# Two lanes of a matmul filler that share a PSUM bank in turn, with a new planned order

## The chip, the cores and the metric

One core of a Trainium2 chip. The metric is the device time of one execution in microseconds (us), as a median over runs. Engines are named as the profile names them: PE (TensorE matmul), PEld (TensorE weight load), DVE (VectorE), ACT (ScalarE), POOL (GpSimd), SP (SyncE, which here issues every transfer).

## The reference

An attention layer and a gated layer run on the same x (2048 rows of 512) and are mixed row by row:

```python
q = (x @ wq), 32 heads of 16;  k = x @ wk;  v = x @ wv      # one k and v for all heads
a = softmax(q k^T / 4) v @ wo
b = (sigmoid(x @ w_gate) * (x @ w_up)) @ w_down             # F = 1792
g = sigmoid((x * gate_w).sum(-1))
out = g * a + (1 - g) * b
```

All is float32. To keep that precision with fast matmuls the kernel splits numbers into a high and a low float32r part and adds three products (high x high, high x low, low x high).

## The kernel before, in words

Rows of x come in 4 blocks (b) of 512. Attention is done in 32 units (u): a block and 4 heads. A unit has 64 matmuls for the row maxima of the scores (kind m, `maximum`, line 1092, reduced by DVE in line 1094), 64 for the scores themselves (kind s, `scores`, line 1101; ACT's exp in line 1103 makes a tile p), and 16 value steps V (`pv`, line 977): four f32 matmuls of 32 columns each, one from each of four p tiles. The maxima of a unit are turned by one small TensorE step T (`max_turn`, line 963) and sent by SyncE into the rows 62, 63, 126 and 127 of the queries (`send_max`, line 970), so that the scores come out with their maximum taken off. `load_q` (line 951) loads a unit's queries in six transfers.

m and s use only 64 rows of the array, so TensorE is split into two **lanes**, rows 0 to 63 and 64 to 127, which run two matmuls at once. Each step of that kind is a *pair slot*. The rest of the work fills the free lanes (kind f, `fill`, line 1071): the gated layer's gate (g) and up (u) products, its down product (d), and the attention's output product (a, at the end e). Each such job is one output tile, or two, in PSUM; there are 8 banks, held by whatever works in them.

Before the change each lane works in a bank of its own:

- For g and u a job is 256 columns of F; lane h makes columns h. It needs all 512 rows of the product's inner dimension and has only 64 partitions, so it also needs the other half of x's rows on its own partitions. `turn_x` (lines 775 to 781) sends x's halves across into tiles xs, by two transfers for each two chunks.
- For d and a a job is one tile of 128 rows of the output. Each lane adds up its half of the inner dimension, so one tile ends in two banks. `part_of` (line 1040) takes them out: the first copy goes to the tile ba by ACT ("first"), later ones go to ACT and then a POOL add (`add_part`, "apart", lines 1052 and 1055), or to a DVE sum onto ba ("sum", line 1034).

After a unit's value steps, `finish` (line 984) copies the bank to ou or, when the run of V steps was cut short, to a partial sum that POOL adds (`add_sums`, line 991). Then SyncE handles the softmax's denominators: `store` (lines 999 and 1002) writes the row of sums to memory and moves the four heads' 16 rows into vd, `sums` (line 1006) reads the sums back, DVE inverts them, `send_inverse` (line 1014) and `spread` (line 1019) send the inverses over 64 rows, POOL multiplies.

**What sets the order.** A string, `ORDER`, is played through a planner (`State`, lines 101 to 640) that keeps a clock and each engine's load, and writes the list of operations in which all engines then stand. A hexadecimal digit is a pair slot (a lane does nothing, m, s or f), V and T are as above, G is a step of the first projections (128 rows), a dot is a short pause. TensorE changes its form between pair slots and the steps V, T and G; the planner books that with `IN` and `OUT`. SP's transfers stand where the planner thinks that their data is there. All engines work through their lists in order, and only semaphores hold them up.

Of the kernel before, what the change touches and what calls it, by code (L numbers as in the profile page):

```python
# [30 lines left out]
RAW, WB, DB, PB, HB, BA_BUFS = 2, 2, 4, 21, 6, 4  # L31
# [19 lines left out]
IN, OUT, VALUES, TURN = 52, 94, 371, 60  # L51
# [9 lines left out]
LATER = (("load_x", 2), 8000), (("load_x", 3), 8100), (("turn_x", 0, 0), 12200), (("turn_x", 0, 1), 12300)  # L61
FEED_AT = 13700
# [11 lines left out]
class Job:  # L74

    def __init__(self, kind, b, i, n, items=()):
        self.kind, self.b, self.i, self.n = kind, b, i, n

        self.items = items

        self.group = (kind, b, i // NT if kind == "d" else 0 if kind == "a" else i)
        self.key = (kind, b, i)

# [5 lines left out]
def block_jobs(b):  # L89
    out = []  # L90

    def ds(gi):
        f0, f1 = FG[gi]
        items = [("d", b, f) for f in range(f0, f1)]
        if gi == len(FG) - 1 and b + 1 < NB:
            items[1:1] = [("x", b + 1, i) for i in range(KC // 2)]
        return [Job("d", b, gi * NT + t, 6 * (f1 - f0), items if t == 0 else ()) for t in range(NT)]

    for gi, (f0, f1) in enumerate(FG):
        for f in range(f0, f1):  # L100
            out.append(Job("g", b, f, 24, [("g", b, f)]))
            if f == f0 and 0 < gi < len(FG) - 1:
                if gi == 1 and b:

                    out += [Job("a", b - 1, t, 3 * KC, [("a", b - 1, i) for i in range(KC // 2)] if t == 0 else ())
                            for t in range(NT)]
                out += ds(gi - 1)
            out.append(Job("u", b, f, 24, [("u", b, f)]))
# [3 lines left out]
class State:  # L112

    def __init__(self):
# [11 lines left out]
        self.job, self.at, self.bank = [0, 0], [None, None], [None, None]  # L126
# [9 lines left out]
        self.parts, self.out = {}, {}  # L136
        self.x_done = [0] * NB
        self.x_ready, self.x_loaded = [NEVER] * NB, [BEGIN[0], X1_THERE, NEVER, NEVER]
# [19 lines left out]
    def send(self, n, kb):  # L158

        self.on("sp", self.now, n * ISSUE)  # L160
        self.on("dma", self.sp, kb * TEN_KB // 10)
# [40 lines left out]
    def run(self, t):  # L202
# [28 lines left out]
        elif what == "x":  # L231
            self.after(at, "turn_x", *args)
# [12 lines left out]
    def divided(self, u, at):  # L245
# [3 lines left out]
        if u == NU - 2:  # L249
            self.jobs += [Job("e", b, t, 3, [("e", b, 0)] if t == 0 else ()) for t in range(NT)]  # L250
        elif u == NU - 3:
            new = [Job("a", b, t, 3 * (KC - 1)) for t in range(NT)]
# [21 lines left out]
    def event(self, what, args):  # L274
# [7 lines left out]
        elif what == "turn_x":  # L282
            b = args[0]
            self.x_done[b] += 1
            at = self.send(2, 1024)
            if self.x_done[b] == KC // 2:
                self.x_ready[b] = at
        elif what == "send_max":
            self.max_ready[args[0]] = self.send(4, 16)
        elif what == "store":  # L290
            at = self.sums_free[args[0] % OU] = self.send(5, 136) + SAFE
            self.after(at, "sums", *args)
        elif what == "sums":
            self.after(self.send(1, 8) + 2 * SAFE, "invert", *args)
# [4 lines left out]
        elif what == "spread":  # L299
            u = args[0]  # L300
            at = self.send(1, 128)
# [59 lines left out]
    def begins(self, h):  # L361
# [7 lines left out]
        if j.kind == "d" and (j.b, j.i % NT) not in self.parts and min(self.tile_free) > self.now:  # L369
            return False  # L370
        return self.has(j, 0)

    def has(self, j, at):
# [3 lines left out]
        if j.kind == "d":  # L377
            f = FG[j.i // NT][0] + at // 6
# [3 lines left out]
    def can_f(self, h):  # L382
        if self.at[h] is None:
            return self.begins(h)
        return self.has(self.jobs[self.job[h]], self.at[h])

    def issue_f(self, h):
        if self.at[h] is None:
            self.bank[h], self.at[h] = self.take(), 0
        j = self.jobs[self.job[h]]  # L390
        self.acts.append(("f", h, j, self.at[h], self.bank[h]))
        self.at[h] += 1
        self.issued[h] += 1

    def settle(self):
        for h in range(2):
            while self.at[h] is not None and self.at[h] == self.jobs[self.job[h]].n:
                j = self.jobs[self.job[h]]
                second = self.halves.get(j.key, 0)
                self.halves[j.key] = second + 1  # L400
                at, i = self.now + LATE, self.bank[h]
                if j.kind == "g":
                    self.acts.append(("gate", h, j, i))
                    at = self.on("act", at, COPY)
                    tail = TAIL_A + FREE_A
                elif j.kind == "u":
                    slot, free = self.take_h()
                    self.acts.append(("gated", h, j, i))
                    at = self.on("dve", max(at, free), GATED)
                    tail = TAIL + FREE  # L410
# [789 lines left out]
```

## Time and profile before

| what | value |
|---|---|
| median of 3 timed runs | 1601.36 us (1601.09 to 1601.44) |
| the profiled execution, in all | 1598.83 us |
| its span, first to last instruction | 1597.1 us |
| TensorE clock granted | 1.000 |
| PE, busy | 1587.9 us (99%) |
| DVE, busy | 1392.0 us (87%) |
| ACT, busy | 1258.4 us (79%) |
| POOL, busy | 848.0 us (53%) |
| moved by DMA | 102.31 MB |

A PE row's duration includes the time in which a matmul shares the array with the next one; start times, not durations, tell what a step costs. SP is a queue only: its rows are transfers being issued and semaphores being waited for. L numbers are lines of the kernel.

### The profile page before, as it was taken

The page shows a single profiled execution, that of the slowest core. Times are in us where ns is not written, and L with a number is a line of the kernel's source. Part 1 is how long each engine was busy: PE and PEld are TensorE (multiplying, and loading weights), DVE is VectorE, ACT ScalarE, POOL GpSimd, SP SyncE. Part 2 cuts the span into 40 slices and gives each one's busy share as a digit, 9 for nine tenths or more (in the row PEclk, how much of TensorE's full clock was granted, in tenths as well). Part 3 has the DMA queues.
Part 4 walks back from the last instruction along what each step waited for, and adds up shares of the span by engine and source line. Part 5 has one row for each costly group of instructions (what it writes and reads, how often), then busy time and mean ns, then how long its engine had stood idle before and what let it go on. Part 6 is the DMA issues. An engine that isn't in the chain of part 4 may idle for free.

```text
span 1597.1 us, 33902 instructions
## 1 busy us (share of the span) xinstructions
PE 1587.9 (99%) x12918; PEld 998.6 (63%) x12918; DVE 1392.0 (87%) x2372; ACT 1258.4 (79%) x2474; POOL 848.0 (53%) x708
## 2 busy tenths in 40 slices
PE   9999999999999999999999999999999999999998
PEld 7776665665656566566666566666656665656654
DVE  7999998998988989988998898889989998988832
ACT  4268778888878878879878877878987887878896
POOL 4254364558363664375745446454936366536463
PEclk9999999999999999999999999999999999999999
DMA  7621121115111212013411121111502021201111
GB/s 239 216 80 42 42 57 36 45 59 137 29 68 32 75 56 60 18 39 83 111 37 58 39 75 54 55 38 59 137 28 68 32 75 46 71 16 42 34 36 44
DMA packets 54678, 102.31 MB, mean 64 GB/s; under 512 B 18232, under 2 KB 19768, under 8 KB 53492
## 3 DMA queue, kind: packets, MB, share of 16 engines
q1 hardware_dynamic: 54516, 100.16, 21.0%
q8 instruction: 101, 1.65, 0.4%
q14 instruction: 61, 0.50, 0.1%
HBM read 74.05 MB, written 13.09 MB: 55 GB/s over the span
## 4 chain that ended last, share of the span: by engine, by line
PE 98%; ACT 0%; DVE 0%; DMA 0%; POOL 0%; issue 0%; DVEq 0%
PE bank L1071 31%; PE bank L977 29%; PE bank L1092 18%; PE bank L1101 16%; PE bank L838 4%; ACT p L1103 0%; PE bank L963 0%; PE bank L908 0%; DVE ba L1148 0%; DVE ba L1034 0%; DMA wkv_raw<-wkv 0%; POOL wkv_s L732 0%; DVE wkv_stack L869 0%; PE bank L1144 0%; DVEq L1196 0%
## 5 line engine op out<-in xcount | busy, mean ns | idle before, releaser
L1094 DVE TENSOR_REDUCE mx<-bank 128x1 f32<-128x512 f32 x2048 | 1257.4, 681 | 133.8 <-PE bank L1092 80.5
L1103 ACT ACTIVATE p<-bank 128x512 f32<-128x512 f32 x2048 | 1050.1, 652 | 2.6 <-PE bank L1101 0.4
L1101 PE MATMUL bank<-qs,ks 64*128 64x512 f32 x2048 | 698.0, 400 | 0.0
L1092 PE MATMUL bank<-ks,qs 62*128 62x512 f32 x2048 | 686.6, 406 | 0.0
L977 PE MATMUL bank<-p,v_aug 128*32 128x512 f32 x4096 | 491.3, 598 | 0.7 <-ACT p L1103 0.7
L1092 PEld LDWEIGHTS bank<-ks,qs 62*128 62x128 f32 x2048 | 338.4, 184 | 151.3 <-issue 51.1
L1101 PEld LDWEIGHTS bank<-qs,ks 64*128 64x128 f32 x2048 | 345.7, 185 | 105.5 <-ACT p L1103 29.9
L991 POOL TENSOR_TENSOR ou<-ou,ou 128x512 f32<-128x512 f32 x201 | 259.0, 1289 | 204.9 <-ACT ou L984 199.2
L984 ACT COPY ou<-bank 128x512 f32<-128x512 f32 x232 | 140.9, 608 | 266.6 <-PE bank L977 122.2
L1071 PE MATMUL bank<-wd,hl 64*128 64x512 f32 x1344 | 273.5, 393 | 0.0
L977 PEld LDWEIGHTS bank<-p,v_aug 128*32 128x32 f32 x4096 | 107.7, 109 | 232.2 <-issue 188.1
L1071 PEld LDWEIGHTS bank<-wd,hl 64*128 64x128 f32 x1344 | 195.0, 185 | 20.4 <-ACT p L1103 1.7
L1071 PE MATMUL bank<-xs,wg 64*128 64x512 f32 x672 | 203.2, 393 | 0.0
L1071 PE MATMUL bank<-xs,wu 64*128 64x512 f32 x672 | 199.7, 393 | 0.0
L1071 PE MATMUL bank<-x,wu 64*128 64x512 f32 x672 | 194.5, 391 | 0.0
L1071 PE MATMUL bank<-x,wg 64*128 64x512 f32 x672 | 190.4, 391 | 0.0
L1071 PEld LDWEIGHTS bank<-xs,wg 64*128 64x128 f32 x672 | 119.7, 185 | 8.1
L1071 PEld LDWEIGHTS bank<-xs,wu 64*128 64x128 f32 x672 | 118.6, 185 | 7.3
L1071 PEld LDWEIGHTS bank<-x,wu 64*128 64x128 f32 x672 | 115.5, 185 | 10.7 <-issue 1.7
L1071 PEld LDWEIGHTS bank<-x,wg 64*128 64x128 f32 x672 | 113.3, 185 | 9.4 <-POOL wu L814 0.8
L1055 POOL TENSOR_TENSOR ba<-ba,pa_d 128x512 f32<-128x512 f32 x48 | 61.8, 1288 | 95.9 <-DVE ba L1034 62.6
L813 POOL CAST wu<-ru 128x1024 fp32r<-128x1024 f32 x27 | 28.1, 1039 | 117.6 <-PE bank L1071 94.3
(83 smaller groups left out, 1064.1 us busy)
## 6 DMA issues: line engine op xcount, KB each, us to landing
rg<-wg SPq DMA_DIRECT2D x28, 512.0 KB
ru<-wu SPq DMA_DIRECT2D x28, 512.0 KB
rd<-wd SPq DMA_DIRECT2D x28, 512.0 KB
qs<-qd SPq DMA_DIRECT2D x192, 64.0 KB
qd<-q SPq DMA_DIRECT2D x32, 256.0 KB
xs<-x SPq DMA_DIRECT2D x16, 512.0 KB
xf<-x_in SPq DMA_DIRECT2D x16, 256.0 KB
ra<-wo SPq DMA_DIRECT2D x8, 512.0 KB
```

Of the source, the lines that this page charges most:

```text
L813: nc.gpsimd.tensor_copy(WS[item][:, 0, :], raw)
L838: nc.tensor.matmul(ps, w[:, p, part(kc)], X[b, kc][:, q, :], start=i == 0, stop=i == 3 * KC - 1)
L977: nc.tensor.matmul(ps[32 * j:32 * j + 32, :], v_aug[:, c, :], PT.pop((u, c, j)), start=start, stop=stop)
L984: nc.scalar.copy(to, ps)
L991: nc.gpsimd.tensor_tensor(SUMS[u], SUMS[u], PARTS_OF[u].pop(0), op=ALU.add)
L1055: nc.gpsimd.tensor_tensor(BA[b, t], BA[b, t], PA.pop((b, t)), op=ALU.add)
L1071: nc.tensor.matmul(banks[i], l, r, start=at == 0, stop=at == j.n - 1)
L1092: nc.tensor.matmul(banks[i], qs_t[u % 3][r, pr, part(qt)], ks[r, kb * 512:(kb + 1) * 512], start=True, stop=True)
L1094: nc.vector.tensor_reduce(MX[u][:, pr, h, qt, kb:kb + 1], banks[i], axis=AX.X, op=ALU.max)
L1101: nc.tensor.matmul(banks[i], ks[r, part(c)], qs_t[u % 3][r, pr, :], start=True, stop=True)
L1103: nc.scalar.activation(p, banks[i], AF.Exp, scale=0.25)
```

## The change

Lanes now share banks. A job has two output tiles and two banks. Each lane first adds its 64 rows of the inner dimension into its own tile's bank, then *crosses over* and adds its half into the other's, without clearing it. So a lane needs only its own half of x, `turn_x` goes (and the host's layout of w_gate and w_up with it), and a tile of d or a ends in one bank.

A lane may not add into a bank while the other still does. The last matmul of a lane's first half and the first matmul after the crossing are tied by an empty SyncE instruction: it waits for the one, and the other waits for it. The planner books it (`TURN_OVER` on SP, `SEEN_OVER` behind that) and lets no lane cross before. `store` and `sums` use one transfer out to memory and one back for the four heads' rows, in place of four. The T step is a plain matmul with the identity, of 32 columns. There are 29 p tiles where there were 21, since the tiles xs are gone. The planner has new costs for the transfers, and the order string is a new one.

```diff
-RAW, WB, DB, PB, HB, BA_BUFS = 2, 2, 4, 21, 6, 4
+RAW, WB, DB, PB, HB, BA_BUFS = 2, 2, 4, 29, 6, 4
...
-IN, OUT, VALUES, TURN = 52, 94, 371, 60
+IN, OUT, VALUES, TURN = 52, 94, 371, 92
...
-FEED_AT = 13700
+FEED_AT = 12200
+TURN_OVER, SEEN_OVER = 40, 100
...
-        return [Job("d", b, gi * NT + t, 6 * (f1 - f0), items if t == 0 else ()) for t in range(NT)]
+        return [Job("d", b, gi * 2 + t, 6 * (f1 - f0), items if t == 0 else ()) for t in range(2)]
...
     def can_f(self, h):
-        if self.at[h] is None:
+        at, n = self.at[h], self.job[h]
+        if at is None:
             return self.begins(h)
-        return self.has(self.jobs[self.job[h]], self.at[h])
+        j = self.jobs[n]
+        if at == j.n and j.kind != "e" and self.now < self.half_end.get((n, 1 - h), NEVER):
+            return False
+        return self.has(j, at % j.n)
...
+        if at + 1 == j.n and not alone:
+            self.half_end[n, h] = self.on("sp", self.now + LATE, TURN_OVER) + SEEN_OVER
...
-    "GGGGGGG555G55G555.G551G554.G..G55G555G55GG555G55G5ff7ffddff7f5ffffff7fdff7ffdff5G55GTG555G577Gbfed9fedbf6fb7edeb"
+    "GGGGGGG555G55G555.G55........5G55GG555GGG555G55G555GG55G557G777fddfffdffdfd7GT7dffff7ffd75Gdefffdfe7edef6f6f9fbf"
...
-    def turn_x(b, i):
-
-        two = XR.pop((b, i))
-        xs = fp.tile([P, 2, 2, TB], F32R, tag="xs", name=f"xs{b}_{i}", bufs=KC // 2)
-        XS[b, 2 * i], XS[b, 2 * i + 1] = xs[:, 0], xs[:, 1]
-        nc.sync.dma_start(f32(xs[TOP]), f32(two[BOT]))
-        nc.sync.dma_start(f32(xs[BOT]), f32(two[TOP]))
...
-        nc.tensor.transpose(ps[:16, :P], mm, ident)
+        nc.tensor.matmul(ps[:32, :P], mm, ident, start=True, stop=True)
...
-        for j in range(4):
-            r = 64 * (u % 2) + DH * j
-            nc.sync.dma_start(VD[u // 2][0][r:r + DH, :], ou[32 * j:32 * j + DH, :])
+        SUMS[u] = dp.tile([4, TB], F32, name=f"sd{u}"), dp.tile([P, TB], F32, name=f"od{u}")
+        nc.sync.dma_start(SUMS[u][0], ou.rearrange("(j r) t -> j r t", j=4)[:, DH, :])
+        nc.sync.dma_start(SUMS[u][1], ou)
...
+        nc.sync.dma_start(rc, sd.rearrange("j (p c) -> (j p) c", c=DH))
+        r = 64 * (u % 2)
+        nc.sync.dma_start(VD[u // 2][0][r:r + 64, :], od.rearrange("(j r) t -> j r t", j=4)[:, :DH, :])
...
+    def after(one, other):
+
+        tc.add_manual_dep(one.ins, other.ins.name, mybir.DependencyInfo(
+            mybir.DependencyClass.Sync, mybir.DependencyReason.DATA), reason="a bank's other rows")
+
+    def fill(h, j, x, at, start, stop, i):
         c, (p, q) = at // 3, THREE[at % 3]
         half = HALF[h]
         if j.kind in "gu":
-            l, r = WS[j.key][half, p, part(c)], (X if c % 2 == h else XS)[j.b, c // 2][half, q, :]
+            l, r = WS[j.key][half, p, part(2 * c + x)], X[j.b, c][half, q, :]
...
-        nc.tensor.matmul(banks[i], l, r, start=at == 0, stop=at == j.n - 1)
+        ins = nc.tensor.matmul(banks[i], l, r, start=start, stop=stop)
+        if at == 0 and not start:
+            after(ins, CROSS.pop((j.key, x)))
+        elif at == j.n - 1 and not stop:
+            CROSS[j.key, x] = nc.sync.nop()
+            after(CROSS[j.key, x], ins)
```

First place: TensorE in block 1, at the end of the first down product's first half (wd is its weights, hl its input; L1139 and L1148 are m and s of the changed kernel, L1113 the filler). Before, both lanes end the same tile's two banks, 72 and 75, and wait for no one:

```order
L1071 MATMUL bank_72<-wd_1_1_6644,hl_3_5969 128x512
L1071 MATMUL bank_75<-wd_1_1_6644,hl_3_5969 128x512
L1071 MATMUL bank_72<-wd_1_1_6644,hl_3_5969 128x512
L1071 MATMUL bank_75<-wd_1_1_6644,hl_3_5969 128x512
L1092 MATMUL bank_76<-ks,qs_109 128x512 [waits DVE_49]
L1092 MATMUL bank_74<-ks,qs_109 128x512 [waits Activation_49]
L1101 MATMUL bank_77<-qs_107,ks 128x512 [waits Activation_49]
L1071 MATMUL bank_75<-wd_1_1_6644,hl_3_5969 128x512
```

After, bank 76 gets the last matmul of its first half in the first row here, and the other lane's first one, which waits for SyncE, seven rows later:

```order
L1113 MATMUL bank_76<-wd_1_1_6603,hl_3_5890 128x512
L1113 MATMUL bank_74<-wd_1_1_6603,hl_3_5890 128x512
L1148 MATMUL bank_72<-qs_107,ks 128x512 [waits DVE_49]
L1113 MATMUL bank_74<-wd_1_1_6603,hl_3_5890 128x512
L1139 MATMUL bank_79<-ks,qs_109 128x512 [waits Activation_49]
L1113 MATMUL bank_74<-wd_1_1_6603,hl_3_5890 128x512
L1148 MATMUL bank_77<-qs_107,ks 128x512 [waits Activation_49]
L1113 MATMUL bank_76<-wd_0_0_6531,hl_0_5499 128x512 [waits SP_sequencer_49]
```

Two rows are a pair slot, so the crossing stands four slots behind. The empty SyncE instruction itself is not among the rows that this view prints.

Second place: TensorE around the eleventh T (L963 before, L998 after; L977 and L1012 are the V steps, four rows each). Before, one V stands on either side:

```order
L1071 MATMUL bank_75<-wd_1_1_6644,hl_3_5969 128x512
L977 MATMUL bank_78<-p_6_0_0_6760,v_aug 32x512 [waits DVE_49]
L977 MATMUL bank_78<-p_6_0_1_6737,v_aug 32x512
L977 MATMUL bank_78<-p_6_1_0_6719,v_aug 32x512
L977 MATMUL bank_78<-p_6_1_1_6713,v_aug 32x512
L963 MATMUL bank_79<-consts,mm_6705 16x128 [waits Activation_49]
L977 MATMUL bank_78<-p_7_0_0_6780,v_aug 32x512
L977 MATMUL bank_78<-p_7_0_1_6797,v_aug 32x512
L977 MATMUL bank_78<-p_7_1_0_6769,v_aug 32x512
L977 MATMUL bank_78<-p_7_1_1_6777,v_aug 32x512
L1101 MATMUL bank_73<-qs_107,ks 128x512 [waits DVE_49]
```

After, two V follow the T (and two stand ahead of it, of which the last two rows are shown):

```order
L1012 MATMUL bank_74<-p_5_1_0_6585,v_aug 32x512
L1012 MATMUL bank_74<-p_5_1_1_6660,v_aug 32x512
L998 MATMUL bank_75<-consts,mm_113 32x128 [waits DVE_49,Activation_49]
L1012 MATMUL bank_74<-p_6_0_0_6632,v_aug 32x512
L1012 MATMUL bank_74<-p_6_0_1_6703,v_aug 32x512
L1012 MATMUL bank_74<-p_6_1_0_6628,v_aug 32x512
L1012 MATMUL bank_74<-p_6_1_1_6695,v_aug 32x512
L1012 MATMUL bank_74<-p_7_0_0_6657,v_aug 32x512
L1012 MATMUL bank_74<-p_7_0_1_6714,v_aug 32x512
L1012 MATMUL bank_74<-p_7_1_0_6650,v_aug 32x512
L1012 MATMUL bank_74<-p_7_1_1_6707,v_aug 32x512
L1148 MATMUL bank_79<-qs_107,ks 128x512
```

The run of V steps between pair slots has four where it had two.

Third place: SyncE, an early unit's sums (sd and od are in memory, ou, rc and vd on the chip). Before:

```order
L999 DMA sd_2327<-ou_1630 4x512 [waits DMAHW7_49,Pool_49]
L1002 DMA vd_1691<-ou_1630 16x512 [waits DMAHW0_49]
L1002 DMA vd_1691<-ou_1630 16x512 [waits DMAHW1_49]
L1002 DMA vd_1691<-ou_1630 16x512 [waits DMAHW2_49]
L1002 DMA vd_1691<-ou_1630 16x512 [waits DMAHW3_49]
L724 DMA rd_3_2393<-wd 128x2x512 [waits DMAHW6_49,DMAHW4_49,Pool_49]
L1006 DMA rc_2407<-sd_2327 128x16 [waits DMAHW7_49,DMAHW5_49]
```

After:

```order
L1034 DMA sd_2326<-ou_1651 4x512 [waits DMAHW1_49,Pool_49]
L1035 DMA od_2327<-ou_1651 128x512 [waits DMAHW2_49]
L1040 DMA rc_2392<-sd_2326 128x16 [waits PE_49,DMAHW3_49,DMAHW1_49]
L1042 DMA vd_1521<-od_2327 64x1x512 [waits DMAHW4_49,DMAHW2_49]
L1050 DMA rd_2465<-rc_2392 128x16 [waits DMAHW6_49,DVE_49]
```

Four transfers into vd became one into od and one back, and the second waits for the first to land.

More of the change, by code (lines that the diff above doesn't have):

```diff
@@ L160, in send, with issue @@
         self.on("sp", self.now, n * ISSUE)
+        self.on("dma", self.sp, kb * TEN_KB // 10)
+        return max(self.sp + SMALL, self.dma + LAST)
+    def issue(self, cost, kb):
+        self.on("sp", self.now, cost)
         self.on("dma", self.sp, kb * TEN_KB // 10)
@@ L368, in begins @@
             return self.ready.get(j.key, NEVER) <= self.now and self.x_ready[j.b] <= self.now
[L369 to L370 removed]
+        first = lambda j, x: j.kind == "d" and (j.b, tile_at(j, x)) not in self.parts
+        if first(j, h):
+            need = 1 + sum(first(self.jobs[m], x) for m, x in self.banks_of if m in (n - 1, n))
+            if sum(at <= self.now for at in self.tile_free) < need:
+                return False
         return self.has(j, 0)
```

274 lines of the change are left out of this document (148 added, 126 removed).

## The prediction, made before the change was run

> **What bounds the kernel now.** I read the page first: busy times and the chain that ended last.
>
> ```profile
> span 1597.1 us, 33902 instructions
> ...
> PE 1587.9 (99%) x12918; PEld 998.6 (63%) x12918; DVE 1392.0 (87%) x2372; ACT 1258.4 (79%) x2474; POOL 848.0 (53%) x708
> ...
> PE 98%; ACT 0%; DVE 0%; DMA 0%; POOL 0%; issue 0%; DVEq 0%
> ```
>
> TensorE is busy for 99% of the span and is 98% of the chain. Busy alone proves little, because a stretched matmul is also busy. So the next view is who waited for whom, of TensorE's matmuls alone; its columns are total us, times, longest us.
>
> ```profile
> PE bank L861 <- POOL v_aug L854: 1.3, 1, 1.3
> PE bank L838 <- POOL wkv_s L732: 1.0, 1, 1.0
> PE bank L1139 <- DVE on L1137: 0.8, 1, 0.8
> PE bank L977 <- ACT p L1103: 0.7, 1, 0.7
> ```
>
> These four are all of it: 3.8 us in 1597. A wait removed on another engine therefore buys nothing by itself. What can change the time is the number of things that TensorE does, what each costs, and new waits. So I price the steps of its order. First a stretch that holds pair slots only, as one row of the windows view:
>
> ```profile
> 98.00:107.00 9.00, 9.00 (x80) 7.85 (x80) 8.72 (x15) 8.96 (x19) 6.79 (x7) 1.00 0.27 83
> ```
>
> 80 matmuls touch these 9 us. One pair hangs over each edge, so about 39 pair slots start in them: **0.23 us a slot**, at a granted clock of 1.00. Next the value steps V, as two rows of the chain in order of time (start us, us, what). A V is eight matmul instructions.
>
> ```profile
> 94.21 3.57 PE bank L977 x32
> 472.11 4.43 PE bank L977 x40
> ```
>
> Four V take 3.57 us and five take 4.43, so **one V costs 0.86 us**. Last the change between the two kinds, from TensorE's timeline around a run of five V and around the end of another run:
>
> ```profile
> 471.71 0.40 PE L1071 MATMUL bank<-x,wu 64*128 64x512 f32 x1
> 472.04 4.50 PE L977 MATMUL bank<-p,v_aug 128*32 128x512 f32 x40
> 476.47 0.50 PE L1101 MATMUL bank<-qs,ks 64*128 64x512 f32 x1
> ```
> ```profile
> 97.71 0.50 PE L1071 MATMUL bank<-x,wg 64*128 64x512 f32 x1
> 98.05 0.40 PE L1101 MATMUL bank<-qs,ks 64*128 64x512 f32 x2
> ```
>
> From the last pair to the first V it is 0.33 us where a slot is 0.23: 0.10 over. From 472.04 to 476.47 it is 4.43, where five V are 4.30: 0.13 over. From the first pair behind a run to the second it is 0.34: 0.11 over. So **going into a run of full-height steps and back costs 0.34 us**, however long the run is.
>
> **The change part by part.** I counted both order strings.
>
> *Steps.* Pair slots go from 4258 to 4256; V, T and G stay at 512, 32 and 24. Runs of V, T or G between pair slots go from 239 to 210 (the second place in the section on the change shows one that grew). That is 29 round trips less: 29 x 0.34 = **-9.9 us**. The two slots are 2 x 0.23 = **-0.5 us**. All of this is on the path, because TensorE is the path. What makes longer runs possible is that a V needs four finished p tiles, and there are 29 buffers for them instead of 21.
>
> *The turn of the maxima (T).* It is a transpose now and becomes a plain f32 matmul with 32 columns, of the form that a V has. TensorE's timeline around one:
>
> ```profile
> 541.40 1.06 PE L977 MATMUL bank<-p,v_aug 128*32 128x512 f32 x8
> 542.40 0.28 PE L963 MATMUL bank<-consts,mm 128*16 128x128 f32 x1
> 542.61 1.06 PE L977 MATMUL bank<-p,v_aug 128*32 128x512 f32 x8
> 543.60 0.50 PE L1101 MATMUL bank<-qs,ks 64*128 64x512 f32 x1
> ```
>
> From 541.40 to 543.60 it is 2.20 us for V, T, V and the way out. Two V and the 0.13 are 1.85, so a T behind a V costs 0.35 us, and one at the head of a run 0.21 (542.40 to 542.61). In before's string 26 stand behind a V and 6 do not: 26 x 0.35 + 6 x 0.21 = 10.4 us. The new T is in no row. The nearest is the V: eight instructions for four f32 matmuls, so two passes of 512 columns, 0.43 us each; two passes of 128 columns are a quarter, 0.22 us, with no change of form to the V beside it. 32 x 0.22 = 7.0, so **-3.4 us**. From below: the T fills one of the four column groups that a V fills, and if the others go on beside it, it may cost half, 0.11: -6.9 us. From above: the old price for one pass, 0.35, and 0.21 for the second, 0.56 each: +7.5 us. I take the V's row.
>
> *Fewer evictions of the down products.* A tile's product leaves one bank instead of two. The planned list goes from 80 to 52 copies on ScalarE, from 84 to 32 sums on VectorE and from 64 to 35 adds on GpSimd. Longer V runs also take 20 partial sums away.
>
> ```profile
> L1034 DVE SCALAR_TENSOR_TENSOR ba<-bank,gom,ba 128x512 f32<-128x512 f32 x64 | 47.3, 739 | 6.1 <-PE bank L1071 3.4 <-PE bank L1101 2.7
> L1052 ACT ACTIVATE pa_d<-bank,gom 128x512 f32<-128x512 f32 x48 | 36.4, 758 | 0.6 <-PE bank L1071 0.3 <-PE bank L1092 0.2
> L1055 POOL TENSOR_TENSOR ba<-ba,pa_d 128x512 f32<-128x512 f32 x48 | 61.8, 1288 | 95.9 <-DVE ba L1034 62.6
> L984 ACT COPY ou<-bank 128x512 f32<-128x512 f32 x232 | 140.9, 608 | 266.6 <-PE bank L977 122.2 <-issue 73.8 <-POOL wd L731 12.5
> L991 POOL TENSOR_TENSOR ou<-ou,ou 128x512 f32<-128x512 f32 x201 | 259.0, 1289 | 204.9 <-ACT ou L984 199.2 <-DMA vd<-ou 3.8
> ```
>
> VectorE loses 52 x 0.74 = 38 us, ScalarE 28 x 0.76 + 20 x 0.61 = 33, GpSimd 49 x 1.29 = 63. Each lies beside TensorE's work now, so I count **0**. If this cover were gone, those engines would be late; they get freer, not fuller.
>
> *SyncE.* Its share of the change in rows: transfer issues with min/median/max ns, the wait for one landing, and an empty instruction.
>
> ```profile
> L999 SPq DMA_DIRECT2D sd<-ou x31: 522/544/2154, 146.4 to 1555.4; - x31
> L1002 SPq DMA_DIRECT2D vd<-ou x124: 553/583/2224, 147.0 to 1557.8; - x124
> L1038 SPq DMA_DIRECT2D out<-ba x12: 338/357/526, 503.9 to 1291.5; - x12
> L1019 SPq DMA_DIRECT2D bc<-rd x31: 577/592/607, 158.0 to 1563.2; - x31
> L1019 SPq EVENT_SEMAPHORE  x23: 17/17/17, 210.3 to 1562.1; - x23
> L780 SPq DMA_DIRECT2D xs<-x x8: 550/1094/1982, 30.7 to 1129.4; - x8
> L951 SPq DMA_DIRECT2D qs<-qd x192: 302/418/2406, 18.4 to 1464.4; - x192
> L970 SPq DMA_DIRECT2D qs<-mt x128: 620/634/785, 76.4 to 1543.3; - x128
> SPq L1019 <- DMA rd<-rc: 27.3, 22, 3.5
> ```
>
> Per unit, four issues of 0.58 give way to one of a whole 128x512 tile (like out, 0.36) and one that reads 64 rows back (like bc, 0.59): 2.33 against 0.95, 31 times, 43 us of SyncE's time. The 16 transfers of turned x go too. Nothing of that is on the path today: **0**. But 192 empty instructions now are, since a matmul waits for each.
>
> *The hand-over.* When a lane's half of a job is done, an empty SyncE instruction waits for its last matmul, and the other lane's first matmul into that bank waits for it. Queued behind that matmul is all of TensorE's order, so a late answer stops everything. In after's order 147 of the 192 hand-overs leave four pair slots from the start of the last matmul to that of the waiting one, 4 x 0.23 = **0.93 us**; 45 leave five or six. What has to fit in: the matmul's 0.39 us (the next row), SyncE's start behind it (the timeline: a pair ends at 561.79 + 0.50 = 562.29, the transfer that waited for it starts at 562.32), and the 17 ns of an empty instruction.
>
> ```profile
> L1071 PE MATMUL bank<-wd,hl 64*128 64x512 f32 x1344 | 273.5, 393 | 0.0
> ```
> ```profile
> 561.79 0.50 PE L1101 MATMUL bank<-qs,ks 64*128 64x512 f32 x1
> 562.32 0.80 SPq L951 DMA_DIRECT2D qs<-qd  x2
> ```
>
> That is 0.39 + 0.03 + 0.02 = 0.44, so 0.49 us is left for the way from SyncE to TensorE, which no row here shows. The same kind of step in the other direction takes 0.03. I take it to fit: **0 us**; from above, a return as long as the slowest ordinary queue-holder, 0.79 (L970), would be 0.30 too long. The Trainium skill's "Perfetto Trace Analysis", section "Sequencer-only Instruction (DRAIN, etc)", says that such a row leaves out the spreading of the semaphore's update behind the instruction; by that the 17 ns are not the whole price. No run here shows it yet, and the third rival is what it would make of the time.
>
> The queue is the other half: SyncE answers in order. Counting after's order, 23 of the 192 stand within four slots behind a transfer's issue (9 behind a weight load, 8 behind a store, 6 others), and 71 within ten. At the medians above the hand-over's 0.49 us covers what is left of such an issue; at the maxima (2.15, 2.41) it does not. I take two of the 23 as losing a microsecond each, **+2 us**; from below 0, from above ten.
>
> **Sum.** -9.9 - 0.5 - 3.4 + 2 = -11.8 us. The profiled execution has a span of 1597.1 and took 1598.83 us in all, so it would be about 1587.0. The median of the three timed runs, 1601.36, lies 2.5 us above the profiled one; the same difference from there is **1589.6 us**.
>
> **The rivals.**
>
> *SyncE's queue is the new wait.* An empty instruction stands behind a transfer that itself waits. For it: the row of L1019 above, where SyncE stood 22 times for a landing, 1.24 us on average, up to 3.5; the new read-back of the sums (vd<-od) waits for a landing too, and with it whatever is behind. The Trainium skill's "Perfetto Trace Analysis", section "DMA Instruction — HWDGE (DVE, Sync)", speaks of "a surprisingly long delay especially when the write target is HBM"; the trace agrees by that row. Against it: the plan books the read-back behind a margin, and only 23 stand close. Ten of these at 1 us instead of two: 1597.6 us.
>
> *The order is planned too tightly for the other engines.* VectorE is 87% busy, and longer V runs take p tiles in lumps. Then rows of TensorE waiting for VectorE or ScalarE appear. Against it: before's 3.8 us of waits with fuller engines. At 8 us: 1597.6 us.
>
> *T costs its upper bound*: 10.9 more, 1600.5 us.
>
> *The hand-over does not fit (slower).* If the way back takes more than 0.49 us, every job stops TensorE. Both lanes hand over in one stretch, so one stop serves both: 96 jobs. At 0.65 us that is 96 x 0.16 = 15 us, 1604.9; at 0.79 it is 96 x 0.30 = 29 us, 1618. About 0.12 us beyond the point (96 x 0.12 = 11.5) eats the gain. Against it: 0.03 us the other way.
>
> **How the numbers follow.** A difference of 0.2%, 3.2 us, is about what a measurement can tell from none. Chances: the forecast 0.60, with a range of its own from 1585 to 1594 (T's lower bound and no late answer; two more late ones); SyncE's queue 0.20; other engines 0.08; T 0.05; the hand-over 0.07. Range: **1585 to 1601**, which leaves out most of the last case and some of the second. Faster by over 0.2% (below 1598.2): the forecast's 0.60, 0.15 of the second, 0.06 of the third, 0.01 of T: 0.82. Within: 0.11. Slower: 0.07.
>
> **What will show it.** Right: TensorE's waits for SyncE next to nothing, slots still 0.23 us and V 0.86, the T's timeline at 0.2 us between two V, and 30 round trips less in the count of V runs. Wrong: rows of TensorE idle behind SyncE's empty instruction; if these lie behind L1034 or L1042 of the changed kernel it is the queue, if they are spread evenly over all jobs it is the way back.

## The result, and the profile after

The changed kernel takes **1588.48 us** as a median of 4 runs (1587.96 to 1589.17), the kernel before 1601.22 in the runs beside it (1600.54 to 1601.44). The ratio is 0.9921, with a 95% interval from 0.9904 to 0.9939: faster by 12.7 us. The forecast was 1589.6.

The profiled execution of the changed kernel took 1589.17 us in all. Its page, with the span, the engines' busy times and the shares of the chain that ended last:

```profile
span 1587.0 us, 33642 instructions
...
PE 1578.4 (99%) x12950; PEld 1026.2 (65%) x12950; DVE 1357.7 (86%) x2320; ACT 1233.2 (78%) x2426; POOL 788.7 (50%) x662
...
PE 95%; ACT 3%; DVE 1%; SPq 0%; DMA 0%; issue 0%; POOL 0%; DVEq 0%; ACTq 0%
```

TensorE is still the path; ScalarE's 3% (0% before) are mostly the exps of L1150, and these come up again among the late pair slots below. All that TensorE's matmuls wait for, by whom (total us, times, longest us):

```profile
PE bank L896 <- POOL v_aug L886: 1.3, 1, 1.3
PE bank L870 <- POOL wkv_s L772: 0.8, 1, 0.8
PE bank L1186 <- DVE on L1184: 0.7, 1, 0.7
PE bank L1012 <- ACT p L1150: 0.3, 1, 0.3
PE bank L1113 <- SPq L1117: 0.3, 1, 0.3
PE bank L1139 <- DMA qs<-qd: 0.2, 1, 0.2
```

That is 3.6 us, as much as before (3.8). The new wait, on SyncE's empty instruction L1117, appears once, though 192 hand-overs are made:

```profile
L1117 SPq EVENT_SEMAPHORE  x192: 17/17/17, 76.3 to 1549.0; - x192
```

The price of each kind of step is what it was. A stretch of pair slots in the windows view, and a run of four V and one of five as rows of the chain:

```profile
98.00:107.00 9.00, 9.00 (x80) 6.27 (x74) 8.98 (x16) 6.35 (x13) 8.68 (x10) 1.00 0.18 59
```
```profile
205.07 3.57 PE bank L1012 x32
286.75 4.43 PE bank L1012 x40
```

80 matmuls in 9 us again, so 0.23 us a slot, and 4.43 - 3.57 = 0.86 us a V. What has changed is how many steps there are, how often TensorE changes its form between them, and the T. TensorE's timeline at the place of the second listing in the section on the change, two V on either side of a T:

```profile
536.67 1.92 PE L1012 MATMUL bank<-p,v_aug 128*32 128x512 f32 x16
538.41 0.27 PE L998 MATMUL bank<-consts,mm 128*32 128x128 f32 x1
538.42 0.63 PE L1012 MATMUL bank<-p,v_aug 128*32 128x512 f32 x3
538.52 0.27 PE L998 MATMUL bank<-consts,mm 128*32 128x128 f32 x1
538.63 1.88 PE L1012 MATMUL bank<-p,v_aug 128*32 128x512 f32 x13
540.44 0.50 PE L1148 MATMUL bank<-qs,ks 64*128 64x512 f32 x1
```

From 536.67 to 540.44 it is 3.77 us; four V and the way out are 3.57 (the first row of the chain above), so this T costs 0.20, a little less than the 0.22 that the prediction took from the V's row. Three matmuls of the next V start at 538.42, ahead of the T's second pass at 538.52: the other column groups do go on beside it, but the run as a whole gains next to nothing from that, and the lower bound of 0.11 isn't reached.

I sorted every step's start in both traces, with a slot at 0.232 us, a V at 0.858 and the way out of a run at 0.138. The two spans are 10.1 us apart:

| where | before | after | difference | in the prediction |
|---|---|---|---|---|
| going into a run and back (runs without G) | 224 runs, 80.4 us | 196 runs, 71.8 us | -8.6 | -9.9, for 29 |
| T, beyond its run's V (31 of 32) | 9.9 us | 6.3 us | -3.6 | -3.4 |
| two pair slots fewer, 0.23 each | 4258 | 4256 | -0.5 | -0.5 |
| pair slots over 0.27 us, their excess | 11, 0.7 us | 31, 2.5 us | +1.8 | +2 |
| from the span's start to the first pair slot, and through the steps G | 71.0 us | 71.5 us | +0.5 | - |
| behind the last step's start, to the span's end | 9.6 us | 10.6 us | +1.0 | - |

The rows add up to -9.4; 0.7 us lies in pieces too small to name. The medians are 12.7 apart, not 10.1: before's profiled execution (1598.83) is a quick one of its kind, after's (1589.17) the slowest of its four.

### The profile page after: what moved, and what is told of

It is laid out like the page before. It is cut to its first block, busy times and chain, and to the rows that moved or that the text cites. A ratio compares the mean times of both kernels' runs of the same rounds, so it can differ in the third digit from the quotient of the medians.

```text
span 1587.0 us, 33642 instructions
## 1 busy us (share of the span) xinstructions
PE 1578.4 (99%) x12950; PEld 1026.2 (65%) x12950; DVE 1357.7 (86%) x2320; ACT 1233.2 (78%) x2426; POOL 788.7 (50%) x662
## 4 chain that ended last, share of the span: by engine, by line
PE 95%; ACT 3%; DVE 1%; SPq 0%; DMA 0%; issue 0%; POOL 0%; DVEq 0%; ACTq 0%
PE bank L1113 32%; PE bank L1012 29%; PE bank L1139 17%; PE bank L1148 14%; PE bank L870 3%; ACT p L1150 2%; SPq L986 0%; PE bank L998 0%; DVE mx L1141 0%; PE bank L1191 0%; DMA qs<-qd 0%; ACT x L796 0%; DVE x L802 0%; DMA wkv_raw<-wkv 0%; ACT q L965 0%
## 5 line engine op out<-in xcount | busy, mean ns | idle before, releaser
L1150 ACT ACTIVATE p<-bank 128x512 f32<-128x512 f32 x2048 | 1035.4, 665 | 4.9 <-PE bank L1148 1.0
L1148 PE MATMUL bank<-qs,ks 64*128 64x512 f32 x2048 | 725.8, 396 | 0.0
L1139 PE MATMUL bank<-ks,qs 62*128 62x512 f32 x2048 | 674.6, 409 | 0.2 <-DMA qs<-qd 0.2
L1012 PE MATMUL bank<-p,v_aug 128*32 128x512 f32 x4096 | 486.7, 597 | 0.3 <-ACT p L1150 0.3
L1139 PEld LDWEIGHTS bank<-ks,qs 62*128 62x128 f32 x2048 | 334.5, 184 | 152.7 <-issue 51.9
L1148 PEld LDWEIGHTS bank<-qs,ks 64*128 64x128 f32 x2048 | 361.9, 185 | 77.1 <-ACT p L1150 31.2
L1026 POOL TENSOR_TENSOR ou<-ou,ou 128x512 f32<-128x512 f32 x181 | 233.3, 1290 | 283.8 <-ACT ou L1019 277.2
L1019 ACT COPY ou<-bank 128x512 f32<-128x512 f32 x212 | 129.7, 612 | 279.4 <-PE bank L1012 136.5
L1113 PE MATMUL bank<-x,wu 64*128 64x512 f32 x1344 | 272.1, 391 | 0.3 <-SPq L1117 0.3
L1012 PEld LDWEIGHTS bank<-p,v_aug 128*32 128x32 f32 x4096 | 122.4, 109 | 230.1 <-issue 192.4
L1113 PE MATMUL bank<-wd,hl 64*128 64x512 f32 x1344 | 271.0, 391 | 0.0
L1113 PE MATMUL bank<-x,wg 64*128 64x512 f32 x1344 | 269.2, 391 | 0.0
L1113 PEld LDWEIGHTS bank<-x,wu 64*128 64x128 f32 x1344 | 201.5, 185 | 18.3 <-issue 1.7
L1113 PEld LDWEIGHTS bank<-wd,hl 64*128 64x128 f32 x1344 | 200.3, 185 | 17.0 <-issue 0.8
L1113 PEld LDWEIGHTS bank<-x,wg 64*128 64x128 f32 x1344 | 199.4, 185 | 16.8 <-issue 1.2
L845 POOL CAST wg<-rg 128x1024 fp32r<-128x1024 f32 x27 | 28.1, 1039 | 137.8 <-PE bank L1113 64.2
L772 POOL TENSOR_TENSOR wd<-rd,wd 128x512 fp32r<-128x512 f32 x56 | 72.3, 1291 | 4.5
L772 POOL TENSOR_TENSOR hl<-h,hl 128x512 fp32r<-128x512 f32 x56 | 72.0, 1286 | 4.5
L1113 PE MATMUL bank<-wa,o 64*128 64x512 f32 x360 | 70.0, 392 | 0.0
```

The source lines that it names most:

```text
L772: lo.tensor_tensor(hl[:, 1, :], raw, f32(hl[:, 0, :]), op=ALU.subtract)
L845: nc.gpsimd.tensor_copy(WS[item][:, 0, :], raw)
L1012: nc.tensor.matmul(ps[32 * j:32 * j + 32, :], v_aug[:, c, :], PT.pop((u, c, j)), start=start, stop=stop)
L1019: nc.scalar.copy(to, ps)
L1026: nc.gpsimd.tensor_tensor(SUMS[u], SUMS[u], PARTS_OF[u].pop(0), op=ALU.add)
L1113: ins = nc.tensor.matmul(banks[i], l, r, start=start, stop=stop)
```

## The experiments

Eleven kernels. Differences of under 2 us between medians are within what the intervals leave open. The base was timed beside the next three kernels alone; the kernel before, timed in each of the three groups, took 1600.35, 1599.88 and 1599.85 us, so a difference over the base from another group carries some 0.5 us more.

**The changed kernel again**, as the base for the kernels sent with it.

> The changed kernel once more, unchanged, to have its time beside the next three on one chip. Theory (fewer changes of TensorE's form, a cheaper turn T, a hand-over that fits): 1588.5 us, 12 to 13 below the kernel before. A rival that the first measurement was a lucky one would put it at 1592 or more.

1588.65 us (1588.15 to 1590.25, 5 runs), before 1600.35; ratio 0.9932, interval 0.9918 to 0.9945.

**The T turned back**, in the changed kernel:

```diff
-        nc.tensor.matmul(ps[:32, :P], mm, ident, start=True, stop=True)
+        nc.tensor.transpose(ps[:16, :P], mm[:, :16], ident)
```

> The changed kernel with one part undone: the turn of the maxima T is a transposition of 16 columns again, the order of everything is kept. Theory: T is on the path, and the profiles show 0.35 us for a transposition behind a V and 0.23 at the head of a run against 0.20 for the plain matmul; 19 stand behind a V and 13 do not, so 19 x 0.15 + 13 x 0.03 = 3.2 us slower than the changed kernel, about 1591.7. Rival (the wait for the maxima hides T): no difference, 1588.5.

1590.08 us (1589.74 to 1592.58), ratio 0.994 (0.9928 to 0.9953): 1.4 us over the base, with intervals that overlap. The span is 1587.9, 1.9 over the base's 1586.0. The trace says more than the medians; TensorE's timeline at the same T:

```profile
537.05 1.92 PE L1012 MATMUL bank<-p,v_aug 128*32 128x512 f32 x16
538.90 0.28 PE L998 MATMUL bank<-consts,mm 128*16 128x128 f32 x1
539.11 1.92 PE L1012 MATMUL bank<-p,v_aug 128*32 128x512 f32 x16
540.96 0.49 PE L1148 MATMUL bank<-qs,ks 64*128 64x512 f32 x1
```

The same stretch now takes 3.91 us instead of 3.77, 0.14 more for one T behind a V. In the changed order 19 T stand behind a V and 13 at the head of a run, where both forms cost about 0.2; 19 x 0.14 = 2.7 us is what undoing it should cost there, less than in before's order with its 26. The sign is as expected; the timed size is not resolved. Sorted by step as in the table, the 31 T take 9.1 us here and 6.4 in the base, 2.8 more, and some of that is made up elsewhere: the slots over 0.27 us take 0.6 less, the end of the span 0.8 less.

**The T alone**, in the kernel before: the same line of code, its 32-column tiles `mm_t` and the reduction that fills them, nothing else.

```diff
...
-        nc.tensor.transpose(ps[:16, :P], mm, ident)
+        nc.tensor.matmul(ps[:32, :P], mm, ident, start=True, stop=True)
```

> The kernel before with that part alone: T is a plain f32 matmul of 32 columns, nothing else changes. Theory: 26 stand behind a V, 26 x 0.15 + 6 x 0.03 = 4.1 us faster than before, about 1597.1. Rival (T gains only together with the new order): 1601.2.

1596.61 us (1595.95 to 1597.72, 11 runs), ratio 0.9978 (0.9969 to 0.9987): **3.7 us faster**, where the prediction has 3.4. The trace has the same 3.7: the 31 T go from 9.9 to 6.2 us. This part is settled by itself.

**Runs split**: the changed kernel with one or more V moved out of 29 runs to the next slots, so that 239 runs are left as before the change; slots, V, T, banks and hand-overs as they are. Only the string is edited:

```diff
-    "7b7b7bbdfedef97bf9fbffeeaaVV555VVV7b7b7bfbdedbdbf9fededededbf7bfb76fef67effd9VVVV5b7b7bfbfe7eeddbf6fedeedef7f6fe"
+    "7b7b7bbdfedef97bf9fbffeeaaVV55V5VV7b7b7bfbdedbdbf9fededededbf7bfb76fef67efVVfd9VV5b7b7bfbfe7eeddbf6fedeedef7f6fe"
...
```

> The changed kernel with 29 runs of V steps split by moving one to three pair slots into them, so that there are 239 runs as before; as many pair slots, V, T and G as in the changed kernel, and shared banks as there. Theory: each round trip costs 0.34 us, 29 x 0.34 = 9.9 us slower than the changed kernel, 1598.4. Rival (the gain comes from the relieved engines and the fewer transfers, and TensorE's changes of form are hidden): within 3 us of the changed kernel, below 1591.5.

1599.06 us (1597.36 to 1599.27), ratio 0.9989 (0.9981 to 0.9998): **10.4 us over the base**, or 0.36 us a round trip. The change keeps its new banks, its fewer evictions of the down products and its fewer transfers, and most of the gain is gone. The split also brings back work on other engines: 27 copies of partial sums on ScalarE (L1019, 212 to 239) and 27 adds on GpSimd (L1026, 181 to 208). The trace tells the two apart: sorted as in the table, going into a run and back takes 9.9 us more for the 29 runs, 0.34 each, while the slots over 0.27 us are fewer than in the base (25 with 1.9 us against 29 with 2.3). So the number of runs is most of the gain; the T's 3.7 is the other part, and new hold-ups take some back.

**Hand-overs one slot closer**: 86 crossings take place three slots behind instead of four or more, by a filler step and its lane's neighbour changing places; the planner's margin is cut to allow it.

```diff
-TURN_OVER, SEEN_OVER = 40, 100
+TURN_OVER, SEEN_OVER = 40, 60
...
-    "7b7b7bbdfedef97bf9fbffeeaaVV555VVV7b7b7bfbdedbdbf9fededededbf7bfb76fef67effd9VVVV5b7b7bfbfe7eeddbf6fedeedef7f6fe"
+    "7b7b7bf9fedef97bf9fbffeeaaVV555VVV7b7b7bfbdedbdbf9fedededef9f7bfb76fef67effd9VVVV5b7b7bfbfe7eeddbf6fedeedfe7f6fe"
...
```

> The changed kernel with the crossing moved one pair slot earlier where a neighbour could change places with it: 86 of the 192 hand-overs leave three slots, 0.70 us, 61 leave four, 45 five or six; as many steps and runs as before. The changed kernel's trace has one hand-over that TensorE waited for: from the last matmul's start to SyncE 0.42 us, 0.02 there, 0.04 back. Theory: 0.48 us is enough, so no cost, 1588.6 (under 1 us more). Rival (the planner's booking of 330 units, 0.77 us, is what the chip needs): 86 hand-overs late by 0.07 and with 0.1 us of weight load uncovered each, 86 x 0.17 / 2 to 86 x 0.17, 7 to 15 us slower.

1588.89 us (1587.22 to 1589.12), ratio 0.9925 (0.9912 to 0.9937), beside before's 1599.88: no cost. 0.70 us is enough, but only just: by the trace's stamps 65 of the weight loads that wait for SyncE start 0.043 to 0.045 us behind the end of its empty instruction, so they were held by it. In the base's order nearly none is.

**Hand-overs two slots closer**: with both constants 0, 62 crossings stand two slots behind and 24 three.

```diff
-TURN_OVER, SEEN_OVER = 40, 100
+TURN_OVER, SEEN_OVER = 0, 0
...
```

> The same with the crossing moved up to two slots: 62 hand-overs leave two slots, 0.46 us, 24 three, 61 four, 45 five or six. Theory: the way takes 0.48 us, so these 62 are late by some 0.02 us and each stop leaves the next weight load uncovered (0.1 us, as in the first pair behind a run): 62 x 0.12 = 7 us at most, half of that where both lanes stop together: 1592 to 1596. Rival (0.77 us needed): 62 x 0.4 = 25 us slower. Rival (less than 0.4 us needed): no cost.

1595.18 us (1593.73 to 1595.73), ratio 0.9965 (0.9953 to 0.9978): **6.5 us over the base**. So a hand-over begins to cost between three slots and two. TensorE's and its weight loads' waits for L1117 in this kernel, and one crossing on the timeline:

```profile
PE bank L1113 <- SPq L1117: 0.4, 1, 0.4
```
```profile
PEld bank L1113 <- SPq L1117: 10.8, 33, 0.8
```
```profile
186.14 0.39 PE L1139 MATMUL bank<-ks,qs 62*128 62x512 f32 x1
186.15 0.78 PE L1113 MATMUL bank<-x,wu 64*128 64x512 f32 x3
186.43 0.19 PEld L1113 LDWEIGHTS bank<-x,wu 64*128 64x128 f32 x2 [0.33 <-SPq L1117]
186.54 0.19 PEld L1148 LDWEIGHTS bank<-qs,ks 64*128 64x128 f32 x1
186.77 0.39 PE L1148 MATMUL bank<-qs,ks 64*128 64x512 f32 x1
```

It is the weight load that waits, not the matmul, so the first row alone would have hidden this. Two slots from 186.14 take 0.63 us instead of 0.46: the crossing itself comes some 0.06 late, and the slot behind it another 0.1, since its weights load late as well. All 62 weight loads at two slots are held by SyncE.

**Four transfers per unit again**: the changed kernel with before's `store` and `sums`, which move the four heads' rows from chip to chip in four transfers.

```diff
-        SUMS[u] = dp.tile([4, TB], F32, name=f"sd{u}"), dp.tile([P, TB], F32, name=f"od{u}")
-        nc.sync.dma_start(SUMS[u][0], ou.rearrange("(j r) t -> j r t", j=4)[:, DH, :])
-        nc.sync.dma_start(SUMS[u][1], ou)
+        sd = SUMS[u] = dp.tile([4, TB], F32, name=f"sd{u}")
+        nc.sync.dma_start(sd, ou.rearrange("(j r) t -> j r t", j=4)[:, DH, :])
+        for j in range(4):
+            r = 64 * (u % 2) + DH * j
+            nc.sync.dma_start(VD[u // 2][0][r:r + DH, :], ou[32 * j:32 * j + DH, :])
...
-        r = 64 * (u % 2)
-        nc.sync.dma_start(VD[u // 2][0][r:r + 64, :], od.rearrange("(j r) t -> j r t", j=4)[:, :DH, :])
...
```

> The changed kernel with the sums' transfers as before the change: one of the row of sums and four of 16 rows each from ou into vd in place of one out to memory and one back; 62 more issues on SyncE, no other edit, the order planned for the short form. Theory (SyncE's queue is on the path once hand-overs go through it): a store then holds SyncE for 0.54 + 4 x 0.58 = 2.9 us instead of 0.9; 22 empty instructions stand within eight slots behind a store, and adding the rows up along the order 13 of them come late, 0.8 us on average: 11 us slower, 1599. Rival (the fewer transfers are worth nothing, as in the trace of before, where no one waited for them): 1588.6.

1603.2 us (1601.59 to 1604.64, 10 runs), ratio 1.0018 (1.0009 to 1.0028): **14.6 us over the base**, slower than the kernel before. Its lines of the filler and the empty instruction are L1112 and L1116. The waits, and SyncE and TensorE at one of them:

```profile
PE bank L1112 <- SPq L1116: 9.9, 13, 1.8
```
```profile
1337.83 2.73 SPq L1037 DMA_DIRECT2D vd<-ou  x3
1340.66 0.18 PEld L1112 LDWEIGHTS bank<-x,wg 64*128 64x128 f32 x1 [2.12 <-SPq L1116]
1340.67 0.49 PE L1112 MATMUL bank<-x,wg 64*128 64x512 f32 x1 [1.76 <-SPq L1116]
```

The empty instruction stands behind issues of the same `store`; 0.1 us after the third one is done, TensorE goes on, and it has stood for 1.76 us. This is the rival of SyncE's queue, seen at work. The rows hold 9.9 of the 14.6 us; by the stamps, 26 slots over 0.27 us whose weight loads start right behind SyncE's answer make up 13.8 (2 slots and 0.6 us in the base). In this order, then, the two fewer issues per unit are what lets the hand-over through SyncE fit. The order was planned for the short form; whether one planned for the four transfers would lose as much wasn't tried, nor the fewer transfers alone in the kernel before.

**VectorE's work put back**: the changed kernel with 52 extra reductions over 128x512, of the size of the 52 sums that went, ahead of 52 of its 84 evictions; their results are not used.

```diff
+    spare_t = cp.tile([P, 1], F32, name="spare")
+    parts_seen = []
...
     def part_of(j, t, i, how):
...
+        k = len(parts_seen)
+        parts_seen.append(how)
+        if (k + 1) * 52 // 84 > k * 52 // 84:
+            nc.vector.tensor_reduce(spare_t, v_aug.rearrange("p c r -> p (c r)"), axis=AX.X, op=ALU.max)
```

> The changed kernel with 52 more reductions of 128x512 on VectorE, one at most of the evictions of the filler's products, in place of the 52 sums that the change took away (their result is used by nothing). About 35 us of work on the fullest of the other engines. Theory: freed engine time is beside the path, a reduction of 0.68 us only shifts VectorE's queue for a while; 0 to 5 us slower, 1589 to 1594. Rival (the gain comes from the freed engines): the whole 12 us or more come back, 1600.

1598.2 us (1597.26 to 1600.72), ratio 0.9989 (0.998 to 0.9998): **9.6 us over the base**, which is near the rival's 1600 and outside the theory's range. The added group, and the chain's shares:

```profile
L1083 DVE TENSOR_REDUCE spare<-v_aug 128x1 f32<-128x512 f32 x52 | 35.0, 673 | 0.0
```
```profile
PE 91%; DVE 7%; ACT 1%; issue 0%; DMA 0%; POOL 0%; DVEq 0%; ACTq 0%
```

VectorE was on 1% of the chain and is on 7%. Sorted by step, the time is scattered: 4.7 us ahead of the first V of a run, 4.0 in pair slots, most of the rest at the start. The 1.9 us ahead of the first pair slot stand in the trace of the hand-overs at three slots too, which cost nothing, so they don't come from the added work. Much of the remainder waits for VectorE: by the stamps, 16 slots over 0.27 us with 2.5 us start right behind its semaphore (3 with 0.2 in the base), and so do 13 first V or T of a run that come over 0.36 us behind the last pair (1 in the base). So time on VectorE is not simply free here. Two readings are left: time that VectorE gets back is worth something, or only that more of it costs. The last three kernels tell these apart.

**Fewer sums, before and after; more work, before.** The kernel before with 52 of its 84 sums made on one column (parts of the down products are missing from the output), the changed kernel with all of its 32 sums so (the same parts missing), and the kernel before with 52 extra reductions like those above, ahead of 52 sums. The edit of the first:

```diff
+    sums_seen = []
...
         if how == "sum":
-            add(banks[i], b, t, scale)
+            k = len(sums_seen)
+            sums_seen.append(t)
+            w = 1 if (k + 1) * 52 // 84 > k * 52 // 84 else D
+            n = b * NT + t
+            nc.vector.scalar_tensor_tensor(BA[b, t][:, :w], banks[i][:, :w], scale[:, n:n + 1], BA[b, t][:, :w],
+                                           op0=ALU.mult, op1=ALU.add)
```

> The kernel before with 52 of its 84 VectorE sums made on one column instead of 512 (so those parts of the down products are missing from the output). The banks are still freed at the same place in VectorE's list; VectorE loses 52 x about 0.68 us = 35 us, as much as the change takes from it in this kind of work. Theory (the prediction's: TensorE is the path, and time that another engine gets back counts 0): within 1.5 us of the kernel before, since all of TensorE's waits there are 3.8 us. Rival (VectorE's time presses on TensorE already, at the rate at which it did when 52 reductions were put into the changed kernel, 9.6 us for about 36 us, a quarter): 9 us faster, about 1591.

> The changed kernel with all of its 32 VectorE sums made on one column instead of 512 (parts of the down products are missing from the output): VectorE loses 32 x about 0.68 = 22 us. Theory (TensorE is the path; what is already in time does not help by being earlier): within 1.5 us of the changed kernel. Rival (VectorE's time counts at a quarter in both directions): 5 us faster, about 1583.

> The kernel before with 52 extra VectorE reductions of 128x512 ahead of 52 of its 84 sums, results unused: VectorE goes from 1392 to about 1428 us. Theory (a full VectorE has no cover left, in this order as in the changed one): 6 to 14 us slower, 1606 to 1614. Rival (only the changed kernel's order is so tight; before's has room): within 3 us.

Beside before's 1599.85 us (15 runs): **1599.1** for before with narrow sums (ratio 0.9996, 0.9987 to 1.0005), **1588.08** for after with narrow sums (0.9926, 0.9912 to 0.9939; the base was 0.9932), **1613.19** for before with more work (1.0081, 1.0067 to 1.0095). Their busy times, and the chain of the last:

```profile
PE 1588.2 (99%) x12918; PEld 998.7 (63%) x12918; DVE 1366.2 (86%) x2372; ACT 1258.6 (79%) x2474; POOL 848.4 (53%) x708
```
```profile
PE 1576.2 (99%) x12950; PEld 1023.7 (65%) x12950; DVE 1342.5 (85%) x2320; ACT 1232.4 (78%) x2426; POOL 788.9 (50%) x662
```
```profile
PE 1599.4 (99%) x12918; PEld 991.4 (62%) x12918; DVE 1420.0 (88%) x2424; ACT 1261.8 (78%) x2474; POOL 848.2 (53%) x708
...
PE 90%; DVE 8%; ACT 1%; issue 0%; DMA 0%; SPq 0%; POOL 0%; DVEq 0%
```

VectorE lost 25.8 us before (1392.0 to 1366.2; I had expected 35, but a sum over one column still takes about 0.21 us) and 15.2 after, and no time clear of the noise came of it in either: 0.8 and 0.6 us, where a quarter would be some 6 and 4 (the second lies little beyond what the intervals leave open). With 35 us of reductions put in, 13.3 us were lost before, and 9.6 after. VectorE's busy time grew by 28 us in both (to 1420.0 from 1392.0, and in the changed kernel to 1385.7 from 1357.3), about as much as the narrow sums took away before. The two directions are not alike: freed work is worth nothing that can be told, and added work costs a quarter to two fifths of its 35 us, in both orders. The added reductions stood ahead of evictions, which free banks; other places in VectorE's list were not tried.

## Why the prediction was right, step by step

*Steps and round trips (-9.9, -0.5).* Right. Splitting 29 runs again costs 10.4 us, of which the trace has 9.9 in the going in and back, 0.34 each, as read from before's timeline. In the change itself 28 fewer runs without a G are 8.6 us: at before's mean of 0.36 us they are 10.0, and the 196 runs that stay cost 0.007 us more each, 1.4 in all, most of it ahead of the first V. What made so few runs possible, the 29 p tiles or the rest of the new plan, was not taken apart.

*T (-3.4).* Right: -3.7 as measured alone, -3.6 in the sorted steps. The V was the nearest row, and the price of two passes of 128 columns read from it (0.22) came out at 0.20, behind a V and at the head of a run alike. The rival of the upper bound, 0.56, is refuted.

*Fewer evictions (0).* Right as a term of the sum, as far as was tried: VectorE is 34.3 us less busy (1392.0 to 1357.7), and narrow sums gain nothing. ScalarE's and GpSimd's share were not tried by themselves; that the split kernel, which keeps the fewer evictions, falls back to within 1.3 us of before speaks for 0 there too. What the prediction said of lost cover was thin ("they get freer, not fuller"): with the work put back the new order loses 9.6 us, about as much as its longer runs gain. The order before loses 13.3 by work added to it, so this is not a weakness of the new one; whether so few runs could have been planned with VectorE as full as before wasn't tried.

*SyncE's share (0).* Right for the change as a whole, incomplete as a reason. "Nothing of that is on the path today" held for the kernel before; in the changed one SyncE answers hand-overs, and with before's transfers this order loses 14.6 us. The term belongs to the rival on SyncE's queue, as what keeps it away.

*The hand-over (0).* Right, with a margin that can now be told. In the median of the 192, SyncE's instruction starts 0.42 us behind the start of the last matmul; it takes 0.017. The way back is seen where TensorE stood waiting for the answer, once in this execution:

```profile
559.47 3.26 SPq L986 DMA_DIRECT2D qs<-qd  x5
...
562.14 0.39 PE L1139 MATMUL bank<-ks,qs 62*128 62x512 f32 x1
562.84 0.18 PEld L1113 LDWEIGHTS bank<-x,wu 64*128 64x128 f32 x1 [0.74 <-SPq L1117]
562.84 0.50 PE L1113 MATMUL bank<-x,wu 64*128 64x512 f32 x1 [0.31 <-SPq L1117]
```

The five issues end at 562.73. By the trace's own stamps the empty instruction stands at 562.776 to 562.793 and the weight load starts at 562.835: **0.042 us** back. In all a hand-over needs 0.42 + 0.017 + 0.042 = 0.48 us, up to the start of the weight load. The prediction, and the expectations after it, set this against the distance between the two matmuls, 0.93, and so put the margin too high: in these traces the weights load about a slot ahead of their matmul (with four slots, 0.02 us behind the start of the slot before), so what costs nothing is 0.48 + 0.23 = 0.71 us, three slots. That agrees with the two experiments: at three slots (0.70) the weight loads are just held and nothing is lost, at two (0.46) they come a whole slot late and two slots take 0.17 us more. Of the four slots, one was to spare. The Trainium skill's "Perfetto Trace Analysis", section "Sequencer-only Instruction (DRAIN, etc)", by which the row leaves out the spreading of the update, holds here, with 0.042 us for what is left out, up to the weight load's start. The rival of a hand-over that does not fit is refuted: with four slots it fits.

*SyncE's hold-ups (+2).* The size was right for a partly wrong reason. There is one late answer where I took two of a microsecond: the one above, behind five issues of which one took 1.4 us, and it cost 0.47 in its slot and 0.11 in the next. The other 1.2 us of the +1.8 is mostly something that I had not seen: 19 times the slot behind a crossing starts 0.04 to 0.11 late, 1.3 us together, without a wait in the rows. The stamps show that it is not SyncE: its empty instruction had ended 0.41 to 0.49 us before. Beside the crossing the other lane's weight load waits for ScalarE; in all 19 an exp of L1150 (a tile p, and with it a bank) ends 0.053 to 0.054 us before that weight load starts. So these 1.3 us belong to the prediction's second rival, an order tight for the other engines, at a size far below its 8 us. The read-back that I feared does wait, but nobody stands behind it:

```profile
SPq L1042 <- DMA od<-ou: 8.3, 9, 2.8
```

*The sum.* -11.8 against -10.1 between the profiled executions and -12.7 between the medians. What the sum left out, 0.5 us at the start, 1.0 at the end and the 1.4 of the runs that stay, is small. That 1588.5 lies so near 1589.6 is in part luck, since two errors of opposite sign met: the profiled execution was to take 1587.0 and took 1589.17, 2.2 us more, and the 2.5 us that I added from it to the median are 0.7 the other way in after's runs.

## What to carry to other kernels

Where one engine is the path, price the steps of its own list, and the changes of form between them, from start times in the trace; here 29 round trips and 32 small steps are the whole gain, and what was taken off VectorE, the one engine where it was tried, is nothing in the sum. But that nothing holds in one direction only: work that is added to an engine 86% busy, or to a queue that now answers TensorE, can cost a quarter of its length or more, so ask of each saving whether it pays for another part of the change. A hand-over between engines by an empty instruction is cheap when it has the distance; measure the distance by moving it closer until it costs, and count it to the weight load, which goes ahead of its matmul.

## What the runs showed of the hardware

- Going from matmuls of 64 rows in two lanes to matmuls of 128 rows and 32 columns and back costs 0.34 to 0.36 us a time (the split runs), whatever the length of the run (in the two traces, medians of 0.34 to 0.38 for runs of one to seven V).
- A float32 transposition to 16 columns among 32-column matmuls costs 0.35 us behind one of them and 0.21 ahead of them; the same as a plain matmul of 32 columns is 0.20 in either place.
- TensorE to SyncE to TensorE by semaphores takes 0.48 us from the start of the last matmul to that of the next weight load, 0.39 of which is the matmul itself. From a semaphore's update by SyncE or ScalarE to the weight load that waits for it, it is 0.04.
- Waits of this kind show on the weight load first: 10.8 us there against 0.4 on the matmuls, at a cost of 6.5.
